# Four edits to a spectral transform with a gated feed-forward layer on one core: operand order, pieces of the inverse, the last pair, and the weights' ring

## The chip, the cores and the metric

The kernel runs on one core of one Trainium2 chip. The metric is the device time of one launch in microseconds (us): 2733.29 us as the median of three runs (2729.64 to 2734.06). All inputs and outputs are float32.

## The reference

The input x has 8 sequences of 3008 rows with 256 channels.

```python
X = np.fft.rfft(x, axis=1)
Yr = Xr @ w_r - Xi @ w_i + b_r          # 256 x 256 mixing, complex
Yi = Xr @ w_i + Xi @ w_r + b_i
Yr = np.sign(Yr) * np.maximum(np.abs(Yr) - 0.01, 0.0)   # the same for Yi
y = np.fft.irfft(Yr + 1j * Yi, n=3008, axis=1)
g, val = y @ w_gate, y @ w_val          # 24064 rows, 256 -> 1536
out = (g / (1 + np.exp(-g)) * val) @ w_out               # 1536 -> 256
```

## The kernel before

**Numbers in two parts.** Most products are made of three TensorE matmuls on `float32r` operands: each operand is held as an upper part (a rounded copy, made on ScalarE) and a lower part (the rest, a subtraction on VectorE or GpSimd), and upper x upper, upper x lower and lower x upper are added in PSUM. `PASSES` (L113) lists these as (weight part, data part). A matmul can start only when its part of the data is there, and the lower part is always made last.

**The transform (first some 620 us).** The transform of length 3008 = 47 x 64 is done in stages: `a_mm` (47 points), `b_mm` (64 points, for two of 24 frequencies at a time), mixing with w_r and w_i, shrinking, `bi_mm` (back over 64), `ai_mm` (back over 47). 96 steps, one for each pair of frequencies of each sequence, are overlapped: each function is recorded with a due time (`put(t, fn)`, step s plus an offset), and `go` issues the functions in the order of these times. Each engine then works through its own instructions in that order, and so does the queue of SyncE (SP), which starts all DMAs. In step s the order on TensorE is `b_mm` (s+0.23), `mix_mm` of the step before, `sum_mm` (s+1.0), `bi_mm` of an earlier step, and the `b_mm` of the next. The mixing takes three products instead of four: `sum_mm` multiplies Xr+Xi with w_r, VectorE adds the biases (`add_bias`), and `mix_mm` adds the two others, with w_i - w_r and -(w_i + w_r). These weights are made on the chip: `load_mix` reads w_r and w_i, `make_mix(0)` to `make_mix(2)` split them and their sums (`wm_hi`, `wm_lo`). The first sequence's `a_mm` results go through DRAM (`a_store`, then `load_a`).

**The layer.** 24 blocks of twice 512 rows (twice 384 in the last two) pass through six pairs of gate and value units. Both products, up and down, are made by Strassen's scheme in Winograd's form: seven products of blocks instead of eight, each of three matmuls. `gate_or_value` issues one unit: seven up products (`up`) into banks b1, b2, b3, and between them the down products of the pair before (`down`). The gate goes through Silu on ScalarE (`take`), the value is multiplied in on VectorE, and the four hidden blocks H11, H12, H22, H21 and four differences T1 to T4 are split by `upper` (ScalarE) and `lower` (GpSimd, or VectorE where named so). Up weights come by DMA, seven blocks for each unit, into a ring of four tiles (`wup`), which lies at the right end of SBUF. Down weights (`wdn`) stay in SBUF.

**Pieces of the inverse.** Six of eight sequences are finished before the layer starts. For the other two, 32 pieces of `ai_mm` (`inverse`, eight short matmul records each) are issued in the layer, in gate units, after the up product 7 and ahead of the up product 3. They use bank b1, from which Silu reads H11 just before, and ScalarE copies the result out (`xt2`).

**The end.** After the last pair nothing is left to lie beside its down products: H21 and T1 to T4 are split, seven products follow, and `result` adds them up into four output blocks, each stored by its own DMA.

Of the kernel before, what the change touches and what calls it, by code (L numbers as in the profile page):

```python
# [43 lines left out]
FIRST_X = {2: -0.93, 3: -0.90, 4: -0.5}  # L44
W_FIRST, W_STEP = 2, 4.2
WARM = 5
GAPS = {1: (0.38,), 2: (0.38, 0.78), 3: (0.38, 0.78, 0.90), 4: (0.38, 0.40, 0.78, 0.90), 5: (0.36, 0.38, 0.40, 0.78, 0.90)}
AFTER = {0.36: 0.62, 0.38: 0.63, 0.40: 0.64, 0.78: 1.03, 0.90: 1.15}

# [59 lines left out]
def f32(ap):  # L109
    return ap.bitcast(F32)  # L110


PASSES = ((0, 0), (0, 1), (1, 0))  # L113


@with_exitstack
def spectral_ffn(ctx: ExitStack, tc: tile.TileContext, xp, w_r, w_i, cb, wup_raw, wdn_raw, ca, cf, ci, co, out):
    nc = tc.nc
    const = ctx.enter_context(tc.tile_pool(name="const", bufs=1))
    dram = ctx.enter_context(tc.tile_pool(name="dram", bufs=2, space=DRAM))  # L120
    wdn = [const.tile([P, NQ, 7, P], F32R, name=f"wdn_{p}") for p in ("hi", "lo")]
    first = ctx.enter_context(tc.tile_pool(name="first", bufs=7, reuse_waits="tile"))
    xt_d = [dram.tile([P, 2, SEQ], F32, name=f"xt_d{b}", bufs=1) for b in range(B)]
    d2 = {b: dram.tile([NK, P, C], F32, name=f"d2_{b}", bufs=1) for b in range(B)}
    wup_d = [dram.tile([P, 2, 7 * P], F32, name=f"wup_d{u}", bufs=1) for u in range(2 * NQ)]
    front = ctx.enter_context(tc.tile_pool(name="front", bufs=1))
    ps_ = ctx.enter_context(tc.tile_pool(name="ps", bufs=1, space=PSUM))
    tail = ExitStack()
    last = tail.enter_context(tc.tile_pool(name="last", bufs=2, side="right"))
    one = ExitStack()  # L130
    ffn = FFN(ctx, tc, first, front, ps_, co, wdn, wup_d, xt_d, d2, out)
    engines = {nc.tensor.engine, nc.vector.engine, nc.scalar.engine, nc.gpsimd.engine}
    with tc.manual_schedule(engines=engines):
        with tc.manual_schedule(engines={nc.sync.engine}):
            go = transform(one, tc, front, last, tail, ffn, ps_, xp, w_r, w_i, cb, wup_raw, wdn_raw, ca, cf, ci, co, wdn, wup_d, xt_d, d2)
        ffn.run(go, one)


def transform(ctx, tc, front, last, tail, ffn, ps_, xp, w_r, w_i, cb, wup_raw, wdn_raw, ca, cf, ci, co, wdn, wup_d, xt_d, d2):
    nc = tc.nc  # L140
    v, act, g = nc.vector, nc.scalar, nc.gpsimd

# [75 lines left out]
    def weight_unit(i, at):  # L218
        kind, u = ("up", i) if i < 2 * NQ else ("down", i - 2 * NQ)
        src = wup_raw[u] if kind == "up" else wdn_raw[u]  # L220
        e = scratch[:, 2 * T : 3 * T].bitcast(I32)
        w = scratch[:, : 2 * T].rearrange("p (a b) -> p a b", b=P)
        a = w[:, 0:4, :].rearrange("p a b -> p (a b)")
        m = w[:, 4:8, :].rearrange("p a b -> p (a b)")
        box = {}
        high = lambda: box["raw"][:, :, 1]
        low = lambda: box["raw"][:, :, 0]

        def load():
            box["raw"] = last.tile([P, T, 2], I32, name="raw64", tag="z_in", bufs=3)  # L230
            nc.sync.dma_start(box["raw"].rearrange("p a b -> p (a b)"), src)

        steps = (
            lambda: v.tensor_scalar(e, high(), 20, 0x7FF, op0=ALU.logical_shift_right, op1=ALU.bitwise_and),
            lambda: v.tensor_scalar(e, e, 896.0, 1150.0, op0=ALU.max, op1=ALU.min),
            lambda: v.tensor_scalar(e, e, 896.0, float(1 << 23), op0=ALU.subtract, op1=ALU.mult),
            lambda: v.scalar_tensor_tensor(a.bitcast(I32), high(), -(1 << 31), e, op0=ALU.bitwise_and, op1=ALU.bitwise_or),
            lambda: v.tensor_scalar(e, high(), 0xFFFFF, 0x100000, op0=ALU.bitwise_and, op1=ALU.bitwise_or),
            lambda: v.tensor_scalar(m.bitcast(I32), low(), 8, None, op0=ALU.logical_shift_right),
            lambda: v.scalar_tensor_tensor(m, m.bitcast(I32), 2.0**-24, e, op0=ALU.mult, op1=ALU.add),  # L240
            lambda: v.scalar_tensor_tensor(a, m, 2.0**-20, a, op0=ALU.mult, op1=ALU.mult),
        )
        a21, a11, a12, a22, s1, s2, s3, s4 = [w[:, j, :] for j in range(8)]

        def sums():
            g.tensor_tensor(s1, a21, a22, op=ALU.add)
            g.tensor_tensor(s2, s1, a11, op=ALU.subtract)
            g.tensor_tensor(s3, a11, a21, op=ALU.subtract)
            g.tensor_tensor(s4, a12, s2, op=ALU.subtract)

        def upper():
            if kind == "up":
                box["both"] = sb.tile([P, 2, 7, P], F32R, name="both", tag="both", bufs=1)
                box["hi"], box["lo"] = box["both"][:, 0], box["both"][:, 1]
            else:
                box["hi"], box["lo"] = [part[:, u] for part in wdn]
            act.copy(box["hi"], w[:, 1:8, :])

        def lower():
            g.tensor_tensor(box["lo"], w[:, 1:8, :], f32(box["hi"]), op=ALU.subtract)  # L260

        def store():
            if kind == "up":
                nc.sync.dma_start(wup_d[u], f32(box["both"].rearrange("p i n a -> p i (n a)")))

        put(at - 1.5, load)
        for step, t in zip(steps, (0.39, 0.93, 0.96, 1.39, 1.93, 1.96, 2.39, 2.93)):
            put(at + t, step)
        put(at + 3.36, sums)
        put(at + 3.72, upper)  # L270
        put(at + 4.36, lower)
        put(at + 4.8, store)

# [80 lines left out]
    def sum_mm(b, p):  # L354
        ps = st["s", b, p] = ps_.tile([P, T], F32, name="ps_s")
        n = 0
        for cc in range(2):
            for w, x in PASSES:
                nc.tensor.matmul(ps[:, :C], lhsT=st["f", b, p][x][:, 2, cc, :], rhs=wmix[0][w][:, cc, :], start=n == 0, stop=n == 5)
                n += 1  # L360

# [47 lines left out]
    def bi_mm(b, p):  # L409
        parts = st.pop(("y", b, p))  # L410
        ps = st["z", b, p] = ps_.tile([P, T], F32, name="ps_z")
        if p == 0:
            for k in range(2):
                for n, (w, x) in enumerate(PASSES):
                    nc.tensor.matmul(ps[:, k * C : (k + 1) * C], lhsT=wi[w][:, k, :], rhs=parts[x][:, k * C : (k + 1) * C], start=n == 0, stop=n == 2)
        else:
            for n, (w, x) in enumerate(PASSES):
                nc.tensor.matmul(ps, lhsT=wi[w][:, 1, :], rhs=parts[x], start=n == 0, stop=n == 2)

    def z_out(b, p):  # L420
# [123 lines left out]
    put(-0.88, load_bias)  # L544
    put(-0.87, load_inverse)
    put(-0.20, make_mix, 0)
    put(0.84, make_mix, 1)
    put(0.86, make_mix, 2)
    put(-0.98, load_wf, 0)
    put(-0.97, load_mix)  # L550
    put(0.82, make_bias)
    put(0.88, make_inverse)

# [9 lines left out]
class FFN:  # L563
# [1 line left out]
    SUMS = ((4, 0, 1), (6, 2, 4), (5, 2, 0), (7, 3, 6))  # L565
    X_AT = {1: 1, 5: 4, 6: 6, 2: 3, 7: 5, 3: 2, 4: 7}

    def __init__(self, ctx, tc, first, front, ps_, co, wdn, wup_d, xt_d, d2, out):
        self.ctx, self.tc, self.first, self.front, self.ps_, self.co, self.wdn = ctx, tc, first, front, ps_, co, wdn
        self.wup_d, self.xt_d, self.d2, self.out = wup_d, xt_d, d2, out  # L570
        self.units = [n * NQ + q for q in range(NQ) for n in range(2)]
        self.held, self.xs, self.raws, self.made = {}, {}, {}, 0
        self.sb = None

    def open_ring(self):
        self.ring = self.ctx.enter_context(self.tc.tile_pool(name="ring", bufs=RING, side="right", reuse_waits="tile"))

    def load_unit(self, k):
# [35 lines left out]
    def run(self, go, one):  # L614
# [52 lines left out]
        def result(pair):  # L667
# [24 lines left out]
            store(2, 2)  # L692
            yield "after d5"

        ends = {}

        def step(name):
# [6 lines left out]
        def gate_or_value(pair, last, n, k, extra):  # L704
# [4 lines left out]
            m5 = hidden[:, 4 + n, :h]  # L709
            first = last is not None and last["q"] == 0  # L710
            closing = last is not None and last["q"] == NQ - 1

            def up(bank, n_, start):
                weights = [held[k][:, i, A_AT[n_], :] for i in range(2)]
# [63 lines left out]
            if gate:  # L778
                diff(last, T4, H21, T2)
                add(last, 1)  # L780
                if (blk, q) in pieces:
                    inverse()
            up(b2, 3, False)
            take(H22, last_sum)
            take(H12, b2[:, :h])
            done(3)
            if n:
                upper(pair, H22)
                lower(g, pair, H22)
            if gate:  # L790
                upper(last, T4)
                lower(g, last, T4)
# [5 lines left out]
                    step("after d2")  # L798
            if value:
                down(last, 5)  # L800
            up(b3, 4, False)
            take(H21, b3[:, :h])

# [75 lines left out]
                    total.update({n_: room(tag) for n_, tag in zip((3, 2, 5, 4), ("mixb1", "ps_z", "ps_x0", "ps_x1"))})  # L879
                last = pair  # L880
        upper(last, H21)
        lower(g, last, H21)
        for i, a, b in ((T1, H12, H11), (T2, H22, T1), (T3, H22, H12), (T4, H21, T2)):
            diff(last, i, a, b)
            upper(last, i)
            lower(g if i == T3 else v, last, i)
        ends["now"] = result(last)
        for n_ in (1, 3, 2, 5, 6, 4, 7):
            down(last, n_)
            if n_ in SUM_AT:  # L890
                add(last, n_)
            if n_ in (2, 6):
                step(f"after d{n_}")
        step("after d7")
        step("after d5")


_OUT = (P, 2, B * SEQ)
# [43 lines left out]
```

## Time and profile before

| what | value |
|---|---|
| median of three runs | 2733.29 us (2729.64 to 2734.06) |
| the profiled execution | 2734.88 us, its span on the core 2733.1 us |
| mean granted TensorE clock | 0.995 of 2.4 GHz |
| TensorE (PE) busy | 2693.9 us, 13173 matmul records |
| VectorE (DVE), ScalarE (ACT), GpSimd (POOL) busy | 2061.1, 1745.3, 1919.3 us |
| DMA | 493.05 MB, queue busy 55.1% of 16 engines |

In a timeline a row has start and duration in us, engine, line of the source, operation, result<-operands and the count of merged instructions; in brackets stands how long the engine had been idle before it and which instruction ended that. Matmuls overlap, so that the distance of two starts, not the duration, is what one costs. PEld is the loading of weights, which runs under the matmul before it.

### The profile page before, as it was taken

The numbers are of one execution on the slowest core, as the hardware profiler recorded it, in microseconds if no ns is written. First come the engines' busy times: TensorE is split into PE (matmuls) and PEld (weight loads), VectorE is DVE, ScalarE is ACT, GpSimd is POOL, SyncE is SP. The second block draws the span as 40 slices with busy tenths as digits, with TensorE's granted clock in tenths as the row PEclk, the third lists the DMA queues.
The fourth block names the chain that finished last, engine by engine and source line by source line (L and its number), as shares of the span: only waits on it lengthen the run. The fifth ranks groups of instructions, "written<-read, shape, count | busy, mean of one in ns | idle before, by whom it ended". The sixth has DMA issues, their size and how long they took to land. (4 is left out here: it accounts for less than half of the span.)

```text
span 2733.1 us, 39899 instructions
## 1 busy us (share of the span) xinstructions
PE 2693.9 (99%) x13173; PEld 2205.8 (81%) x13173; DVE 2061.1 (75%) x3108; ACT 1745.3 (64%) x3376; POOL 1919.3 (70%) x1460
## 2 busy tenths in 40 slices
PE   8999999999999999999999999999999999999998
PEld 5787878987888887888888888888888888888898
DVE  4888887667777777777777777777777777778787
ACT  5777777776666565656666566656665566565664
POOL 1333333247888788888888878888888888888885
PEclk9999999999999999999999999999999999999999
DMA  8998988873444454445444444445444444444453
GB/s 265 308 297 285 291 253 258 261 244 133 161 163 150 151 166 160 154 140 166 160 153 147 160 166 155 147 164 166 148 147 159 155 149 148 143 165 149 145 182 101
DMA packets 184990, 493.05 MB, mean 180 GB/s; under 512 B 17776, under 2 KB 93680, under 8 KB 184688
## 3 DMA queue, kind: packets, MB, share of 16 engines
q1 hardware_dynamic: 184784, 490.50, 55.1%
q8 instruction: 105, 1.72, 0.3%
q14 instruction: 101, 0.83, 0.1%
HBM read 379.81 MB, written 110.62 MB: 179 GB/s over the span
## 5 line engine op out<-in xcount | busy, mean ns | idle before, releaser
L624 PE MATMUL bank<-x_parts,wup 128*128 128x512 f32 (+1 forms) x6048 | 1552.4, 391 | 0.3 <-DVE bank L753 0.2
L624 PEld LDWEIGHTS bank<-x_parts,wup 128*128 128x128 f32 x6048 | 1128.0, 188 | 249.6 <-DVE bank L753 0.8
L644 POOL TENSOR_TENSOR h_parts<-more,h_parts 128x512 fp32r<-128x512 f32 (+1 forms) x573 | 853.4, 1500 | 140.6 <-ACT h_parts L640 125.4
L644 POOL TENSOR_TENSOR h_parts<-hidden,h_parts 128x512 fp32r<-128x512 f32 (+1 forms) x432 | 556.7, 1294 | 240.4 <-ACT h_parts L640 183.2
L624 PE MATMUL bank<-h_parts,wdn_hi 128*128 128x512 f32 (+1 forms) x2016 | 622.2, 389 | 0.9 <-POOL h_parts L644 0.9
L640 ACT CAST h_parts<-hidden 128x512 fp32r<-128x512 f32 (+1 forms) x432 | 265.4, 614 | 469.7 <-DVE hidden L726 469.7
L665 DVE TENSOR_TENSOR sums<-sums,bank 128x512 f32<-128x512 f32 (+1 forms) x360 | 242.3, 673 | 285.1 <-PE bank L624 284.0
L624 PEld LDWEIGHTS bank<-h_parts,wdn_hi 128*128 128x128 f32 x2016 | 378.6, 188 | 81.4 <-POOL h_parts L644 1.8
L726 DVE TENSOR_TENSOR hidden<-hidden,bank 128x512 f32<-128x512 f32 (+1 forms) x576 | 376.0, 674 | 87.8 <-PE bank L624 71.6
L396 POOL TENSOR_TENSOR t<-t,y 128x512 f32<-128x512 f32 x96 | 122.2, 1273 | 396.6 <-DVE y L393 389.3
L624 PE MATMUL bank<-h_parts,wdn_lo 128*128 128x512 f32 (+1 forms) x1008 | 392.6, 389 | 4.2 <-DVE sums L665 4.2
L640 ACT CAST h_parts<-more 128x512 fp32r<-128x512 f32 (+1 forms) x576 | 350.7, 609 | 21.4 <-DVE more L635 18.3
L724 ACT ACTIVATE hidden<-bank 128x512 f32<-128x512 f32 (+1 forms) x432 | 252.5, 584 | 142.9 <-PE bank L624 131.9
L635 DVE TENSOR_TENSOR more<-hidden 128x512 f32<-128x512 f32 (+1 forms) x288 | 281.5, 1015 | 0.0
L635 DVE TENSOR_TENSOR more<-hidden,more 128x512 f32<-128x512 f32 (+1 forms) x288 | 246.0, 854 | 0.0
L753 DVE TENSOR_TENSOR bank<-hidden,bank 128x512 f32<-128x512 f32 (+1 forms) x288 | 197.0, 684 | 55.9 <-PE bank L624 39.9
L731 ACT COPY bank<-bank 128x512 f32<-128x512 f32 (+1 forms) x288 | 161.6, 561 | 120.0 <-DVE hidden L726 110.5
L624 PEld LDWEIGHTS bank<-h_parts,wdn_lo 128*128 128x128 f32 x1008 | 189.6, 188 | 46.0 <-issue 4.5
L612 POOL TENSOR_TENSOR x_parts<-xf,x_parts 128x512 fp32r<-128x512 f32 (+1 forms) x168 | 211.3, 1278 | 22.0 <-ACT x_parts L611 22.0
L739 ACT COPY hidden<-bank 128x512 f32<-128x512 f32 (+1 forms) x288 | 166.9, 579 | 8.6 <-PE bank L624 0.4
L389 ACT COPY t<-mixb 64x256 f32<-64x256 f32 x384 | 140.7, 366 | 36.4 <-PE mixb L373 32.7
L776 DVE TENSOR_TENSOR hidden<-hidden,bank 128x512 f32<-128x512 f32 (+1 forms) x144 | 97.4, 676 | 56.8 <-PE bank L624 56.4
(95 smaller groups left out, 3153.0 us busy)
## 6 DMA issues: line engine op xcount, KB each, us to landing
wup<-wup_d SPq DMA_DIRECT2D x288, 896.0 KB, 4.7
d<-a SPq DMA_DIRECT2D x128, 192.0 KB, 3.9
a_in<-d SPq DMA_DIRECT2D x96, 256.0 KB, 4.9
d<-z SPq DMA_DIRECT2D x96, 256.0 KB, 4.7
out<-o SPq DMA_DIRECT2D x88, 256.0 KB, 6.2
scratch<-xp SPq DMA_DIRECT2D x116, 192.0 KB, 4.7
z_in<-d SPq DMA_DIRECT2D x48, 384.0 KB, 4.9
xt_d<-xt SPq DMA_DIRECT2D x48, 376.0 KB, 4.1
```

Of the source, the lines that this page charges most:

```text
L389: act.copy(t[64 * half : 64 * half + 64, k * C : (k + 1) * C], mixed[p % 2][64 * k : 64 * k + 64, half * C : (half + 1) * C])
L612: self.tc.nc.gpsimd.tensor_tensor(part[:, 1, :h], src, f32(part[:, 0, :h]), op=ALU.subtract)
L624: nc.tensor.matmul(o, lhsT=weights[w], rhs=parts[x], start=start and i == 0, stop=stop and i == 2, skip_group_check=True)
L635: v.tensor_tensor(at(o, h), at(a, h), at(b, h), op=ALU.subtract)
L640: act.copy(pair[i][:, 0, :h], at(i, h))
L644: eng.tensor_tensor(pair[i][:, 1, :h], at(i, h), f32(pair[i][:, 0, :h]), op=ALU.subtract)
L665: v.tensor_tensor(o, o, spare[:, :h], op=ALU.add)
L724: act.activation(at(i, h), src, AF.Silu)
L726: v.tensor_tensor(at(i, h), at(i, h), src, op=ALU.mult)
L731: act.copy(b3[:, :h], b1[:, :h])
L739: act.copy(m5, b2[:, :h])
L753: v.tensor_tensor(b2[:, :h], m5, b3[:, :h], op=ALU.add)
```

## The change

Five things change.

1. The order of the three matmuls in `sum_mm` and `bi_mm` (`LATE`): those with the lower part of the data come last, in `sum_mm` after both halves of the contraction.
2. At the start w_r and w_i are loaded behind the first `a_in`, and all three sets of mixing weights are made before the first step's other work.
3. The pieces of the inverse are issued one product later, after the up product 3.
4. The last pair's down goes by eight plain products on H11, H22, H12, H21 instead of seven of Strassen's. For that block a21 of the last pair's down weights is kept too (`w21`, 1 KB beside `wdn`), H12 is split as well, its lower part on VectorE.
5. A pad of 864 bytes stands beside the ring, which moves down by as much; `w21` moves what lies left up by 1024 bytes.

```diff
+PAD = 216
+LATE = ((0, 0), (1, 0), (0, 1))
...
+    w21 = const.tile([P, 2, P], F32R, name="w21")
...
             act.copy(box["hi"], w[:, 1:8, :])
+            if i == 3 * NQ - 1:
+                act.copy(w21[:, 0, :], a21)
...
             g.tensor_tensor(box["lo"], w[:, 1:8, :], f32(box["hi"]), op=ALU.subtract)
+            if i == 3 * NQ - 1:
+                g.tensor_tensor(w21[:, 1, :], a21, f32(w21[:, 0, :]), op=ALU.subtract)
...
-        for cc in range(2):
-            for w, x in PASSES:
+        for w, x in LATE:
+            for cc in range(2):
                 nc.tensor.matmul(ps[:, :C], lhsT=st["f", b, p][x][:, 2, cc, :], rhs=wmix[0][w][:, cc, :], start=n == 0, stop=n == 5)
...
-            for n, (w, x) in enumerate(PASSES):
+            for n, (w, x) in enumerate(LATE):
                 nc.tensor.matmul(ps, lhsT=wi[w][:, 1, :], rhs=parts[x], start=n == 0, stop=n == 2)
...
-    put(0.84, make_mix, 1)
-    put(0.86, make_mix, 2)
+    put(-0.18, make_mix, 1)
+    put(-0.16, make_mix, 2)
     put(-0.98, load_wf, 0)
-    put(-0.97, load_mix)
+    put(-0.945, load_mix)
...
     def open_ring(self):
+        self.ctx.enter_context(self.tc.tile_pool(name="pad", bufs=1, side="right")).tile([P, PAD], F32, name="pad")
         self.ring = ...
...
+        def outer(pair, c, n_):
+            h = pair["h"]
+            o = pair.setdefault("o", {})[c, 2] = self.sb.tile([P, T], F32, name="o", bufs=4)[:, :h]
+            v.tensor_tensor(o, pool["sums"][:, SUM_AT[n_], :h], total[5][:, :h], op=ALU.add)
...
             if gate:
                 diff(last, T4, H21, T2)
                 add(last, 1)
-                if (blk, q) in pieces:
-                    inverse()
             up(b2, 3, False)
             take(H22, last_sum)
             take(H12, b2[:, :h])
+            if gate and (blk, q) in pieces:
+                inverse()
...
                 lower(g, pair, H22)
+                if final:
+                    upper(pair, H12)
+                    lower(v, pair, H12)
...
+            if final and n:
+                outer(pair, 1, 6)
             up(b3, 4, False)
...
         upper(last, H21)
-        lower(g, last, H21)
-        for i, a, b in ((T1, H12, H11), (T2, H22, T1), (T3, H22, H12), (T4, H21, T2)):
-            diff(last, i, a, b)
-            upper(last, i)
-            lower(g if i == T3 else v, last, i)
-        ends["now"] = result(last)
-        for n_ in (1, 3, 2, 5, 6, 4, 7):
-            down(last, n_)
-            ...
+        outer(last, 2, 7)
+        lower(v, last, H21)
+        ...
+        def direct(i, f, j):
+            for c in (1, 2):
+                weights = [part[:, q, block[c, f], :] for part in wdn] if (c, f) in block else [self.w21[:, x, :] for x in range(2)]
+                product(bank[c, j][:, :h], weights, [last[i][:, x, :h] for x in range(2)], (c, j, f) == (2, 2, 2), i in (H12, H21))
+
+        def close(c, j, left):
+            v.tensor_tensor(o[c, j], left, bank[c, j][:, :h], op=ALU.add)
+            s = BLOCKS[-1][0] + (h if j == 1 else 0)
+            nc.sync.dma_start(out[:, c - 1, s : s + h], o[c, j])
+
+        direct(H11, 1, 1)
+        direct(H22, 2, 2)
+        direct(H12, 1, 2)
+        close(1, 2, o[1, 2])
+        close(2, 2, o[2, 2])
+        direct(H21, 2, 1)
+        close(1, 1, sums(1))
+        close(2, 1, sums(7))
```

On VectorE, at the start of the program before the change (`wm` are parts of mixing weights, `wsum` their sums, `f` the spectrum of a step, `wi` the inverse's table, `mixb` the bank that the biases open):

```order
L206 TENSOR_TENSOR wm_lo<-wr,wm_hi 128x512
L338 TENSOR_TENSOR f<-ps_b,f 128x256
L344 CAST f_hi<-f 128x256
L347 TENSOR_TENSOR f_lo<-f,f_hi 128x256
L350 TENSOR_TENSOR f_lo<-ps_b,f_hi 128x512
L211 TENSOR_SCALAR bias<-bias 32x256 x2
L201 TENSOR_TENSOR wsum<-wj,wr 128x512
L206 TENSOR_TENSOR wm_lo<-wsum,wm_hi 128x512
L203 TENSOR_TENSOR wsum<-wj,wr 128x512
L204 TENSOR_SCALAR wsum<-wsum 128x512
L206 TENSOR_TENSOR wm_lo<-wsum,wm_hi 128x512
L215 TENSOR_TENSOR wi_lo<-raw_i,wi_hi 128x256
```

The same place after it:

```order
L209 TENSOR_TENSOR wm_lo<-wr,wm_hi 128x512
L204 TENSOR_TENSOR wsum<-wj,wr 128x512
L209 TENSOR_TENSOR wm_lo<-wsum,wm_hi 128x512
L206 TENSOR_TENSOR wsum<-wj,wr 128x512
L207 TENSOR_SCALAR wsum<-wsum 128x512
L209 TENSOR_TENSOR wm_lo<-wsum,wm_hi 128x512
L345 TENSOR_TENSOR f<-ps_b,f 128x256
L351 CAST f_hi<-f 128x256
L354 TENSOR_TENSOR f_lo<-f,f_hi 128x256
L357 TENSOR_TENSOR f_lo<-ps_b,f_hi 128x512
L214 TENSOR_SCALAR bias<-bias 32x256 x2
L218 TENSOR_TENSOR wi_lo<-raw_i,wi_hi 128x256
```

The five instructions of the second and third set of mixing weights moved from behind the first step's spectrum to ahead of it.

On TensorE, `sum_mm` and `bi_mm` of a step of the transform before (`f_lo` and `y_lo` are the lower parts of the data):

```order
L359 MATMUL ps_s<-wm_hi,f_hi 128x256
L359 MATMUL ps_s<-wm_hi,f_lo 128x256
L359 MATMUL ps_s<-wm_lo,f_hi 128x256
L359 MATMUL ps_s<-wm_hi,f_hi 128x256
L359 MATMUL ps_s<-wm_hi,f_lo 128x256
L359 MATMUL ps_s<-wm_lo,f_hi 128x256
L418 MATMUL ps_z<-y_hi,wi_hi 128x512
L418 MATMUL ps_z<-y_lo,wi_hi 128x512
L418 MATMUL ps_z<-y_hi,wi_lo 128x512
```

And after:

```order
L366 MATMUL ps_s<-wm_hi,f_hi 128x256 x2
L366 MATMUL ps_s<-wm_lo,f_hi 128x256 x2
L366 MATMUL ps_s<-wm_hi,f_lo 128x256 x2
L425 MATMUL ps_z<-y_hi,wi_hi 128x512
L425 MATMUL ps_z<-y_hi,wi_lo 128x512
L425 MATMUL ps_z<-y_lo,wi_hi 128x512
```

`f_lo` is now asked for at the fifth of six matmuls instead of the second, and `y_lo` at the third of three instead of the second.

## Rows read from the trace of the kernel before

**Rows 1.** Windows: busy us (count) of PE, PEld, DVE, ACT, POOL; clock; DMA share; GB/s.
```profile
2160.00:2500.00 340.00, 340.00 (x1465) 275.00 (x1464) 263.34 (x367) 210.43 (x378) 288.26 (x208) 1.00 0.44 148
...
42.50:46.00 3.50, 3.22 (x13) 3.01 (x14) 1.78 (x5) 0.73 (x3) 0.00 (x0) 0.51 0.87 255
```

**Rows 2.** Timeline of the start: DMA issues on SP, then PE, then DVE.
```profile
24.55 0.41 SPq L186 DMA_DIRECT2D wj<-w_i  x1
25.07 0.93 SPq L312 DMA_DIRECT2D a_in<-d  x2
...
31.75 2.05 PE L320 MATMUL ps_b<-wf,a_in 128*128 128x128 f32 x8 [2.21 <-DMA a_in<-d]
42.78 0.55 PE L373 MATMUL mixb<-wm_hi,f_hi 128*128 128x256 f32 x1 [3.29 <-DVE mixb L364]
...
34.72 0.42 DVE L338 TENSOR_TENSOR f<-ps_b,f 128x256 f32<-128x256 f32 x1 [3.29 <-ACT f_hi L341]
36.57 0.59 DVE L211 TENSOR_SCALAR bias<-bias 32x256 f32<-32x256 f32 x2
37.19 0.69 DVE L201 TENSOR_TENSOR wsum<-wj,wr 128x512 f32<-128x512 f32 x1
41.61 0.42 DVE L215 TENSOR_TENSOR wi_lo<-raw_i,wi_hi 128x256 fp32r<-128x256 f32 x1
41.94 0.69 DVE L364 TENSOR_TENSOR mixb<-ps_s,bias 128x512 f32<-128x512 f32 x1
```

**Rows 3.** DMA issues: tensors, queue, count, size, median us from issue to landing.
```profile
wj<-w_i SPq DMA_DIRECT2D x1, 256.0 KB, 5.8
```

**Rows 4.** Waits from 60 to 620 us: total us, times, longest.
```profile
PEld ps_z L418 <- DVE y_lo L405: 16.9, 39, 0.9
```

**Rows 5.** Timeline of PE: one `bi_mm` that waits.
```profile
178.75 0.39 PE L418 MATMUL ps_z<-y_hi,wi_hi 128*128 128x512 f32 x1
179.25 0.50 PE L418 MATMUL ps_z<-y_lo,wi_hi 128*128 128x512 f32 x1
179.59 0.40 PE L418 MATMUL ps_z<-y_hi,wi_lo 128*128 128x512 f32 x1
```

**Rows 6.** Timeline round one piece of the inverse: PE, then ACT.
```profile
731.99 1.13 PE L824 MATMUL bank<-w,z 96*128 96x94 f32 x8
...
731.34 0.60 ACT L724 ACTIVATE hidden<-bank 128x512 f32<-128x512 f32 x1 [1.12 <-PE bank L624]
...
733.16 0.48 ACT L833 COPY xt<-bank 128x376 f32<-128x376 f32 x1 [0.71 <-PE bank L824]
```

**Rows 7.** Waits from 650 to 2150 us.
```profile
PEld bank L824 <- ACT hidden L724: 15.5, 32, 0.5
```

**Rows 8.** Timeline of the end: PE, ACT, POOL, DVE.
```profile
2715.99 0.51 PE L624 MATMUL bank<-h_parts,wdn_hi 128*128 128x384 f32 x2
2723.73 0.66 PE L624 MATMUL bank<-h_parts,wdn_lo 128*128 128x384 f32 x1 [4.21 <-DVE sums L665]
...
2715.62 0.52 ACT L640 CAST h_parts<-hidden 128x384 fp32r<-128x384 f32 x1 [1.12 <-DVE hidden L726]
...
2716.21 2.28 POOL L644 TENSOR_TENSOR h_parts<-hidden,h_parts 128x384 fp32r<-128x384 f32 x2 [0.63 <-ACT h_parts L640]
...
2715.03 1.54 DVE L726 TENSOR_TENSOR hidden<-hidden,bank 128x384 f32<-128x384 f32 x3
2716.49 1.14 DVE L635 TENSOR_TENSOR more<-hidden 128x384 f32<-128x384 f32 x1
...
2718.83 0.55 DVE L635 TENSOR_TENSOR more<-hidden,more 128x384 f32<-128x384 f32 x1
...
2728.57 0.55 DVE L675 TENSOR_TENSOR o<-sums,bank 128x384 f32<-128x384 f32 x1
```

**Rows 9.** Groups by line and shape: count, busy us, mean ns of one, idle before.
```profile
L624 PE MATMUL bank<-x_parts,wup 128*128 128x512 f32 x5544 | 1449.8, 396 | 0.3 <-DVE bank L753 0.2
...
L624 PE MATMUL bank<-h_parts,wdn_hi 128*128 128x512 f32 x1848 | 577.4, 393 | 0.0
```

More of the change, by code (lines that the diff above doesn't have):

```diff
@@ L130, in spectral_ffn @@
     one = ExitStack()
-    ffn = FFN(ctx, tc, first, front, ps_, co, wdn, wup_d, xt_d, d2, out)
+    ffn = FFN(ctx, tc, first, front, ps_, co, wdn, w21, wup_d, xt_d, d2, out)
     engines = {nc.tensor.engine, nc.vector.engine, nc.scalar.engine, nc.gpsimd.engine}
@@ L134, in spectral_ffn, with transform @@
         with tc.manual_schedule(engines={nc.sync.engine}):
-            go = transform(one, tc, front, last, tail, ffn, ps_, xp, w_r, w_i, cb, wup_raw, wdn_raw, ca, cf, ci, co, wdn, wup_d, xt_d, d2)
+            go = transform(one, tc, front, last, tail, ffn, ps_, xp, w_r, w_i, cb, wup_raw, wdn_raw, ca, cf, ci, co, wdn, w21, wup_d, xt_d, d2)
         ffn.run(go, one)
-def transform(ctx, tc, front, last, tail, ffn, ps_, xp, w_r, w_i, cb, wup_raw, wdn_raw, ca, cf, ci, co, wdn, wup_d, xt_d, d2):
+def transform(ctx, tc, front, last, tail, ffn, ps_, xp, w_r, w_i, cb, wup_raw, wdn_raw, ca, cf, ci, co, wdn, w21, wup_d, xt_d, d2):
     nc = tc.nc
@@ L413, in bi_mm @@
             for k in range(2):
-                for n, (w, x) in enumerate(PASSES):
+                for n, (w, x) in enumerate(LATE):
                     nc.tensor.matmul(ps[:, k * C : (k + 1) * C], lhsT=wi[w][:, k, :], rhs=parts[x][:, k * C : (k + 1) * C], start=n == 0, stop=n == 2)
         else:
-            for n, (w, x) in enumerate(PASSES):
+            for n, (w, x) in enumerate(LATE):
                 nc.tensor.matmul(ps, lhsT=wi[w][:, 1, :], rhs=parts[x], start=n == 0, stop=n == 2)
@@ L566, with __init__ @@
     X_AT = {1: 1, 5: 4, 6: 6, 2: 3, 7: 5, 3: 2, 4: 7}
-    def __init__(self, ctx, tc, first, front, ps_, co, wdn, wup_d, xt_d, d2, out):
+    def __init__(self, ctx, tc, first, front, ps_, co, wdn, w21, wup_d, xt_d, d2, out):
         self.ctx, self.tc, self.first, self.front, self.ps_, self.co, self.wdn = ctx, tc, first, front, ps_, co, wdn
@@ L572, in __init__ @@
         self.held, self.xs, self.raws, self.made = {}, {}, {}, 0
-        self.sb = None
+        self.w21, self.sb = w21, None
     def open_ring(self):
+        self.ctx.enter_context(self.tc.tile_pool(name="pad", bufs=1, side="right")).tile([P, PAD], F32, name="pad")
         self.ring = self.ctx.enter_context(self.tc.tile_pool(name="ring", bufs=RING, side="right", reuse_waits="tile"))
@@ L711, in gate_or_value @@
             closing = last is not None and last["q"] == NQ - 1
+            final = blk == len(BLOCKS) - 1 and q == NQ - 1
             def up(bank, n_, start):
@@ L881, in run @@
         upper(last, H21)
-        lower(g, last, H21)
-        for i, a, b in ((T1, H12, H11), (T2, H22, T1), (T3, H22, H12), (T4, H21, T2)):
-            diff(last, i, a, b)
-            upper(last, i)
-            lower(g if i == T3 else v, last, i)
-        ends["now"] = result(last)
-        for n_ in (1, 3, 2, 5, 6, 4, 7):
-            down(last, n_)
[L890 to L895, printed above, removed]
+        outer(last, 2, 7)
+        lower(v, last, H21)
+        h, q = last["h"], last["q"]
+        sums = lambda n_: pool["sums"][:, SUM_AT[n_], :h]
+        bank = {(1, 1): total[2], (1, 2): total[3], (2, 1): total[4], (2, 2): spare}
+        block = {(1, 1): A_AT[1], (1, 2): A_AT[2], (2, 2): A_AT[4]}
+        o = last["o"]
+        for c in (1, 2):
+            o[c, 1] = self.sb.tile([P, T], F32, name="o", bufs=4)[:, :h]
+        def direct(i, f, j):
+            for c in (1, 2):
+                weights = [part[:, q, block[c, f], :] for part in wdn] if (c, f) in block else [self.w21[:, x, :] for x in range(2)]
[12 more added lines that the diff above has]
+        close(2, 1, sums(7))
 _OUT = (P, 2, B * SEQ)
```

## The prediction, made before the changed kernel ran

> **What bounds the kernel now.** I read the windows first. In a stretch of the layer where only full products run, PE is busy for 340.00 of 340 us at full clock and gets through 1465 matmuls, one each 0.232 us; DMA is at 0.44 [rows 1]. So the layer, three quarters of the time, is a queue of matmuls without gaps, and only a gap that PE really has, or a cheaper matmul, can be won there. The change leaves the number of matmuls nearly alone (three more of 384 columns at the end), so the rest of the reading was a search for gaps of PE in the places that the edits touch: the timeline of the start [rows 2], the waits of the transform with one timeline [rows 4, 5], the waits of the layer with one piece [rows 6, 7], and the timeline of the end [rows 8]. The reader is to see in each which instruction ends the gap and how much of it PE could have filled.
>
> **Start: mixing weights.** Before, the first mixing matmul stands at 42.78 us, after PE had idled 3.29 us for VectorE's biases, which stand at 41.94. VectorE did the first spectrum from 34.72 to 36.57, the biases' signs (0.59), and then, from 37.19 to 41.61, the two sums of mixing weights with their splitting: 4.4 us, in which it also waits for ScalarE [rows 2]. That block now goes first, from the time w_j lands. It was issued at 24.55 and took 5.8 us [rows 2, 3], so it landed at 30.35; it now stands behind one `a_in`, and `a_in` cannot be issued before the last store has landed. Two issues there took 0.93 us, and 256 KB go by in about 1 us at such a rate, so I put w_j at 31.5. The block then ends at about 36.0, the spectrum takes 1.85 (to 37.9), a wait for ScalarE's copies some 0.2, signs and `wi_lo` 1.0 (0.59 + 0.42), and the biases start at 39.2 to 39.6; the mixing starts 0.84 behind that (as 42.78 behind 41.94), at about 40.2. That is 2.5 us earlier. PE worked at 1.2 GHz from 42.50 to 46.00, busy for 3.22 us [rows 1], after that idle time; without it the same work needs half, 1.6 us less. The first `b_mm`, which waited 2.21 us for `a_in` [rows 2], starts sooner, but its results now wait on ScalarE behind the weights. I take 3.0 us: the 2.5, and a third of the 1.6, because other, shorter idle times are still there. From both sides: 4.1 if the clock stays up all the while, 1.0 if w_j lands 1.5 us later than I put it.
>
> **Transform: the lower part last.** In the stretch 60 to 620 us the loading of `bi_mm`'s second weights waits 39 times for `y_lo`, 16.9 us in all, 0.43 on the mean [rows 4]. One of them: starts at 178.75, 179.25, 179.59 [rows 5], so the second comes 0.50 behind the first where 0.23 is due [rows 1]. With the two last exchanged PE fills this wait with one matmul of 512 columns, 0.232 us, and still waits 0.2 after it. 39 x 0.232 = 9.0 us. In `sum_mm` the new order lets PE start three matmuls of 256 columns more before it asks for `f_lo`. I count that at nothing: VectorE makes `y_lo` right behind `f_lo`, so where `sum_mm` would run on, `bi_mm` waits as much longer for the same `y_lo`. What comes next on PE, `b_mm`, moves up by the 0.232, and the spectrum of the next step with it. The bounds are 0 (VectorE or the DMA queue sets the pace and the time comes back as another wait) and 16.9 (the whole wait). I take 9.0, which is worked out from the rows where it happens.
>
> **Pieces.** 32 times the loading of the inverse's operand waits 0.49 us for Silu on H11 [rows 7] (15.5 / 32), because only one up product, 0.7 us, lies between Silu's input and bank b1's next writer. The timeline shows Silu from 731.34 to 731.94 and the piece at 731.99 [rows 6]. With another product of three matmuls between, 0.7 us, the wait is gone. What PE loses is less than the wait, as some of it lay under the matmul before: the matmul ahead of the piece started at about 731.53, the next was due at 731.76, so 0.23 is seen, and the refilling of the pipeline costs a part of a matmul more. I take 0.28, 32 x 0.28 = 9.0 us, between 7.4 (0.23 each) and 15.5. What is late next: ScalarE's copy out of b1 (0.48) now stands behind both other Silus and ahead of T4's split. The piece takes 0.9 us, and after it PE has two products, 1.4 us, before value's first product writes b1; copy and hand-over need about 0.8 from the piece's end. Some 0.4 to 0.6 are left, and T4 is asked for two products later still. So the copy stays covered.
>
> **End.** Before, PE stands still for 4.21 us until 2723.73 for the chain of differences, and VectorE's last sum starts at 2728.57 [rows 8], 4.5 us before the span's end. Now: H12 is multiplied by 2716.1 (the second of three from 2715.03). ScalarE splits H22 from 2715.62 (0.52) and H12 to 2716.65. VectorE's lower part of H12 runs beside GpSimd's of H22 (two from 2716.21, 2.28 together). Next to GpSimd a VectorE difference took 1.14 us, alone 0.55 [rows 8]; I take 1.14, to 2717.8. Then follow the first outer sum (0.5), H21's product (0.5), the second outer sum, H21's upper part on ScalarE at 2718.85 to 2719.4 and its lower part to 2719.95. PE passes through 24 matmuls at 0.17 to 0.175 ([rows 8]: two take 0.51, of which 0.34 is the second's own) from 2715.8, waits a little for H22's and H21's lower parts, and starts the last at 2720.6. The last sum starts at 2721.3 instead of 2728.57. I take 7.2 us; bounds 6.0 (four stores close together, or ScalarE slower) and 8.0 (the difference takes 0.55).
>
> The Trainium skill ("SBUF — State Buffer", section "Who interferes with whom") says that a VectorE instruction with two SBUF inputs and a GpSimd one that reads SBUF exclude each other, the later one waiting until the other ends; this speaks against giving H12's lower part to VectorE. The 1.14 against 0.55 agrees in kind. By the rule alone the difference would begin only when H22's is done, at 2717.3, and end at 2717.9: the end would win 7.1 instead of 7.2.
>
> **Pad.** The ring and all that lies left move, no instruction does. The ring's matmuls are listed at 396 ns, those with resident weights at 393 [rows 9]; no row shows the ring elsewhere. I take nothing, between 5544 x 3 ns = 17 us won (the ring becomes as the resident ones) and as much lost. The extra splitting of one weight block is one short ScalarE and GpSimd instruction in the transform: nothing, as PE does not wait for it.
>
> **Sum.** 3.0 + 9.0 + 9.0 + 7.2 = 28.2 us off the profiled execution's 2734.88, 2706.7; that execution lies 1.6 above the median of the runs, so the median comes to 2733.29 - 28.2 = 2705.1.
>
> **Rivals.**
> *The pad helps.* If the ring's distance to the resident weights' address matters, the 5544 matmuls fall by 2 to 3 ns each, 11 to 17 us: 2688 to 2694. For it: the 3 ns. Against: these are durations, which overlap, and the data come from other tiles as well. Chance 0.18.
> *The transform keeps its pace.* If the loop over VectorE and ScalarE, or the DMA queue, sets the steps, the 9.0 and most of the 3.0 come back as other waits: 2705 + 11 = 2716. For it: each waiting `bi_mm` follows one long chain on VectorE. Against: PE's next `b_mm`, at which that chain begins again, does move. The same time results, for other reasons, if the copy from b1 comes too late and the pieces win nothing: 2714. Together 0.14.
> *The new place slows the ring.* If weights read from the new address cost more, each of 6048 up matmuls pays: the gains are gone from 28.2 / 6048 = 4.7 ns each, a fiftieth of 0.232; at 8 ns the time is 2705 + 48 = 2753. For it: nothing but that both groups differ by 3 ns. Chance 0.04.
> *The edits do nothing measurable*, since the waits only change names: 2733. Chance 0.03.
>
> **How the numbers follow.** The forecast has 0.61 and its own range is 2698 to 2711. What this kernel's measurement can tell from no change is 0.2%, 5.5 us. The range from 2689 to 2716 takes in most of the pad's case and of the slower transform. Faster: 0.61 + 0.18 + 0.14 = 0.93; same 0.03; slower 0.04.
>
> **What would show it.** The first mixing matmul at about 40 us, and no half clock behind it; the waits for `y_lo` halved, not gone; no wait of the inverse's operand for Silu, and none of value's first product for the copy; less than 1 us of idle PE in the end, and the last sum 7 us sooner; in the stretch of full products still 0.232 us each. The forecast is wrong if this last number moves, if the layer starts less than 8 us sooner, or if value's first product waits.

## The result, and the profile after

The changed kernel takes 2661.47 us (median of four runs, 2658.75 to 2665.69). Its ratio to the kernel before (2732.39 us, now the median of four) is 0.9743, 95% interval 0.9726 to 0.9760. That is 71 us off, where 28 were forecast, and below the range that was given. Of the four terms that were priced, the transform came out at about half its size, the other three near theirs, and together they came near the forecast's sum; the term that was put at zero, the pad, was worth some 46 us.

The windows of the changed kernel, one stretch of full products and the start (columns as in [rows 1]):

```profile
2110.00:2445.00 335.00, 335.00 (x1477) 276.70 (x1476) 269.33 (x371) 208.89 (x377) 287.55 (x208) 1.00 0.45 153
...
42.50:46.00 3.50, 3.50 (x23) 2.69 (x22) 2.34 (x5) 3.07 (x8) 1.27 (x1) 1.00 0.57 159
```

PE was busy without a gap before and is so now, at the same granted clock of 1.00. Yet 1477 matmuls go through in 335 us, one each 226.8 ns, where 1465 took 340 us, 232.1 ns each [rows 1]. In the second row the stretch behind the first mixing now has the full clock. That need not be a gain: the half clock lies elsewhere now, as the account of the start below shows.

The two traces are split at four landmarks that both have: the first `mix_mm`, the first up product, the first up products of 384 columns, the last up product. Timeline of PE, the kernel before (its first `mix_mm` stands in [rows 2]), then after:

```profile
609.46 0.85 PE L624 MATMUL bank<-x_parts,wup 128*128 128x512 f32 x3
...
2580.10 1.91 PE L624 MATMUL bank<-x_parts,wup 128*128 128x512 f32 x9
...
2715.29 0.69 PE L624 MATMUL bank<-x_parts,wup 128*128 128x384 f32 x3
```

```profile
40.30 0.68 PE L380 MATMUL mixb<-wm_hi,f_hi 128*128 128x256 f32 x1
...
599.62 0.86 PE L632 MATMUL bank<-x_parts,wup 128*128 128x512 f32 x3
...
2514.64 1.73 PE L632 MATMUL bank<-x_parts,wup 128*128 128x512 f32 x8
...
2649.82 0.51 PE L632 MATMUL bank<-x_parts,wup 128*128 128x384 f32 x2
```

| stretch | before | after | gain |
|---|---|---|---|
| to the first `mix_mm` | 42.78 | 40.30 | 2.5 |
| from there to the first up product | 566.7 | 559.3 | 7.4 |
| from there to the row that leads into 384 columns | 1970.6 | 1915.0 | 55.6 |
| from there to the last up matmul | 135.5 | 135.4 | 0.1 |
| from the last up matmul to the span's end | 17.5 | 9.1 | 8.4 |

The first two rows are from one execution each, and executions differ there by several us. The first up product starts at 604.5 to 609.5 in the four traces with the old start and transform (before, e1, e2 and e3 of the experiments below), and at 597.5 to 602.1 in those with the new ones, except for e4 with 608.0. The last up matmul is the last of its row (2715.64 and 2650.00); the spans' ends are 2733.1 and 2659.1. Of the 55.6 us, 10.3 lie at the pieces (below). The other 45 are 5.4 ns on each of some 8300 products of 512 columns (5544 and 1848 in [rows 9], and half of the latter again for the lower part of the weights).

Groups by line and shape in the changed kernel, 700 to 2440 us (columns as in [rows 9]):

```profile
L632 PE MATMUL bank<-x_parts,wup 128*128 128x512 f32 x5029 | 1277.7, 389 | 0.0
L632 PE MATMUL bank<-h_parts,wdn_hi 128*128 128x512 f32 x1676 | 516.4, 389 | 0.0
```

Products with resident weights fell from 393 to 389 ns although those weights did not move. Their starts say the same: the three matmuls of such a product started 230.6 and 231.9 ns apart on the mean before, and 226.7 and 226.9 now (all such products in 2130 to 2470 us). A place of the ring that costs something costs it to the matmuls next to the ring's own, too.

The 384-column blocks gained next to nothing. Windows of 100 us there, before and after:

```profile
2590.00:2690.00 100.00, 100.00 (x566) 98.11 (x565) 82.54 (x144) 63.15 (x142) 79.70 (x74) 1.00 0.55 180
```

```profile
2530.00:2630.00 100.00, 100.00 (x569) 98.48 (x568) 82.85 (x145) 63.64 (x143) 79.94 (x74) 1.00 0.56 182
```

176.7 and 175.7 ns each: what the old place cost appears with 512 columns, hardly with 384.

### The profile page after: what moved, and what is told of

It is laid out like the page before. It is cut to its first block, busy times and chain, and to the rows that moved or that the text cites. A ratio compares the mean times of both kernels' runs of the same rounds, so it can differ in the third digit from the quotient of the medians.

```text
span 2659.1 us, 39894 instructions
## 1 busy us (share of the span) xinstructions
PE 2632.8 (99%) x13176; PEld 2201.3 (83%) x13176; DVE 2075.1 (78%) x3101; ACT 1742.5 (66%) x3374; POOL 1919.4 (72%) x1459
## 4 chain that ended last, share of the span: by engine, by line
PE 92%; DVE 4%; ACT 2%; DMA 1%; issue 1%; SPq 0%; POOL 0%; DVEq 0%; ACTq 0%; POOLq 0%
PE bank L632 76%; PE mixb L380 3%; PE ps_a L305 3%; PE ps_x L450 3%; PE ps_b L327 2%; PE ps_z L425 2%; PE ps_s L366 2%; PE bank L843 1%; DVE f_hi L351 1%; DMA scratch<-xp 1%; DVE y_lo L412 1%; DVE f_lo L357 1%; ACT t L396 1%; DVE f_lo L354 0%; ACT f_hi L348 0%
## 5 line engine op out<-in xcount | busy, mean ns | idle before, releaser
L632 PE MATMUL bank<-x_parts,wup 128*128 128x512 f32 (+1 forms) x6048 | 1511.9, 385 | 0.3 <-DVE bank L767 0.2
L632 PE MATMUL bank<-h_parts,wdn_hi 128*128 128x512 f32 (+1 forms) x2014 | 612.3, 385 | 0.0
L740 DVE TENSOR_TENSOR hidden<-hidden,bank 128x512 f32<-128x512 f32 (+1 forms) x576 | 375.9, 674 | 78.2 <-PE bank L632 69.5
L643 DVE TENSOR_TENSOR more<-hidden 128x512 f32<-128x512 f32 (+1 forms) x286 | 288.8, 1048 | 0.0
L643 DVE TENSOR_TENSOR more<-hidden,more 128x512 f32<-128x512 f32 (+1 forms) x286 | 255.3, 893 | 0.0
L380 PE MATMUL mixb<-wm_hi,f_hi 128*128 128x256 f32 x384 | 131.8, 343 | 1.4 <-DVE mixb L371 1.3
```

What stands on the lines that cost most here:

```text
L380: nc.tensor.matmul(mixed[p % 2][:, half * C : (half + 1) * C], lhsT=parts[x][:, q, cc, :], rhs=wmix[i][w][:, cc, :], start=False, stop=(cc ...
L632: nc.tensor.matmul(o, lhsT=weights[w], rhs=parts[x], start=start and i == 0, stop=stop and i == 2, skip_group_check=True)
L643: v.tensor_tensor(at(o, h), at(a, h), at(b, h), op=ALU.subtract)
L740: v.tensor_tensor(at(i, h), at(i, h), src, op=ALU.mult)
```

## The experiments

All times are medians of four to ten runs; each ratio is to the kernel before on the same chip, whose median was 2735.81 beside e1 to e4, 2734.84 beside e5 to e8 and 2734.49 beside e9 to e12.

| run | ring's start, within 256 bytes | inputs and resident weights, within 256 | other edits | us | ratio (95%) |
|---|---|---|---|---|---|
| e1 pad only | 199808, 128 | 128 | none | 2689.97 | 0.9824 (0.9809 to 0.9839) |
| e2 32 bytes | 200640, 192 | 128 | none | 2735.37 | 0.9997 (0.9987 to 1.0007) |
| e3 block only | 200672, 224 | 128 | none | 2735.08 | 0.9999 (0.9989 to 1.0010) |
| e4 no pad | 200672, 224 | 128 | all | 2711.26 | 0.9909 (0.9890 to 0.9927) |
| e5 352 | 200320, 128 | 128 | all | 2662.44 | 0.9734 (0.9719 to 0.9748) |
| e6 608 | 200064, 128 | 128 | all | 2661.51 | 0.9731 (0.9714 to 0.9747) |
| e7 736 | 199936, 0 | 128 | all | 2706.74 | 0.9895 (0.9880 to 0.9909) |
| e8 800 | 199872, 192 | 128 | all | 2709.34 | 0.9904 (0.9889 to 0.9919) |
| e9 | 199936, 0 | 0 | all | 2660.09 | 0.9729 (0.9715 to 0.9744) |
| e10 | 200064, 128 | 0 | all | 2707.00 | 0.9900 (0.9886 to 0.9915) |
| e11 old order | 199808, 128 | 128 | without LATE | 2666.54 | 0.9755 (0.9740 to 0.9769) |
| e12 old mix | 199808, 128 | 128 | without the mix weights' move | 2665.59 | 0.9752 (0.9735 to 0.9768) |

The starts are those that the allocation gives; a ring tile is 7168 bytes, 28 x 256, so all four tiles have the same remainder.

**Which edit, and which address.** The change moves two things: the ring by 864 bytes, and inputs and hidden blocks by 1024 (`w21`). e1 and e3 do one each, e2 tries another pad, e4 leaves the pad out.

```diff
 # e1: the kernel before, and (e2: PAD = 8)
+PAD = 216
+        self.ctx.enter_context(self.tc.tile_pool(name="pad", bufs=1, side="right")).tile([P, PAD], F32, name="pad")
 # e3: the kernel before, and
+    const.tile([P, 2, P], F32R, name="w21")
 # e4: the changed kernel
-PAD = 216
-        self.ctx.enter_context(self.tc.tile_pool(name="pad", bufs=1, side="right")).tile([P, PAD], F32, name="pad")
```

> The kernel before with the pad of 864 bytes alone: the ring starts at byte 199808 of a partition instead of 200672 and all else stays. Theory A (the ring's address makes every product of the layer slow, whichever weights it uses itself): the 512-column products start 227 ns apart instead of 232.4, about 45 us off, near 2688. Theory B (it is the addresses of the inputs, which the new weight block moves up by 1024 bytes): nothing changes, 2732. Theory C (neither alone, both must agree): 2732 here and in the run with the block alone.

> The kernel before with a pad of 32 bytes: the ring starts at 200640, again a multiple of 64, but at another place within 512 and 2048 bytes than with 864. Theory A in the form that the multiple of 64 decides: 2688, as with 864 bytes. Theory A in the form that the distance to the inputs or a place within a larger block decides: the time differs from that of the pad of 864, 2700 to 2735. Theory B: 2732.

> The kernel before with 1024 bytes more below the inputs, as the new weight block takes them; the ring stays at 200672. Theory A: 2732, products 232 ns apart. Theory B: 2688, products 227 ns apart.

> The changed kernel without the pad: the inputs stay 1024 bytes up, the ring is back at 200672. Theory A: the 45 us come back, 2706, which would be the prediction's own number for the other three edits. Theory B: 2661. Theory C: 2706, too, and then the first and third run tell it from A.

One window, 2130 to 2470 us, of e1, e2, e3 and e4 in this order:

```profile
2130.00:2470.00 340.00, 340.00 (x1500) 280.90 (x1500) 273.80 (x377) 215.09 (x387) 291.09 (x210) 1.00 0.45 151
```

```profile
2130.00:2470.00 340.00, 339.95 (x1467) 273.62 (x1466) 263.44 (x368) 209.31 (x376) 283.69 (x205) 1.00 0.45 150
```

```profile
2130.00:2470.00 340.00, 339.95 (x1468) 274.88 (x1467) 263.84 (x368) 209.33 (x376) 284.32 (x205) 1.00 0.45 150
```

```profile
2130.00:2470.00 340.00, 340.00 (x1460) 274.01 (x1459) 264.05 (x369) 207.86 (x372) 282.82 (x205) 1.00 0.45 150
```

Only e1 has 1500 matmuls in 340 us, 226.7 ns each. The pad alone takes 45.8 us off (2735.81 to 2689.97); the block alone and 32 bytes do nothing. Theory A holds, theories B and C fall, and 200640, a multiple of 64, shows that a multiple of 64 is not enough. The count behind PE is the instrument for all that follows. e4 came to 24.6 us less than before, not far from the forecast's sum, 28.2, in which the pad has no part.

**Which remainder counts.** Four pads in the changed kernel, `PAD = 88, 152, 184, 200` (352, 608, 736 and 800 bytes).

> The changed kernel with a pad of 352 bytes: the ring starts at 200320, the same place within 512 bytes as with 864 (128), but another within 1024 and 2048. Theory 128 (a start that is a multiple of 128 is enough), theory 256 (128 within 256) and theory 512 (128 within 512, where the inputs and the resident weights start as well): 2661, products 227 ns apart. Theory 1024 or 2048 (the place within a larger block): about 2711, 232 ns or more.

> The changed kernel with a pad of 608 bytes: the ring starts at 384 within 512 bytes, 128 within 256. Theories 128 and 256: 2661. Theory 512: about 2711.

> The changed kernel with a pad of 736 bytes: the ring starts at 256 within 512 bytes, 0 within 256 and within 128. Theory 128: 2661. Theories 256 and 512: about 2711.

> The changed kernel with a pad of 800 bytes: the ring starts at 192 within 512 bytes, 64 within 128, a multiple of 64 and of nothing larger. All theories that ask for a multiple of 128 or more: about 2711. A theory in which only the places 448 and 480 within 512 bytes, which the kernel before and the run with 32 bytes had, are bad: 2661.

The same window of e6 and of e7:

```profile
2130.00:2470.00 340.00, 340.00 (x1500) 281.06 (x1499) 273.70 (x376) 214.90 (x387) 290.80 (x211) 1.00 0.45 154
```

```profile
2130.00:2470.00 340.00, 340.00 (x1465) 275.13 (x1464) 262.98 (x369) 208.77 (x374) 284.70 (x206) 1.00 0.44 147
```

352 and 608 bytes are as fast as 864, 736 and 800 as slow as none. 608 stands at 384 within 512, so 512 falls; 736 is a multiple of 128, so 128 falls. What is left is 128 within 256 bytes. e7 and e8, with a bad place and all other edits, are 28.1 and 25.5 us below before: again about the sum of the other terms.

**Place or distance.** All of x_parts, h_parts and wdn start at 128 within 256 as well. e9 and e10 put 128 bytes below them, so that they start at 0, and the ring at 0 and at 128.

```diff
 # the changed kernel; e9 with PAD = 184, e10 with PAD = 152
+    const.tile([P, 32], F32, name="shift")
     wdn = [const.tile([P, NQ, 7, P], F32R, name=f"wdn_{p}") for p in ("hi", "lo")]
```

> The changed kernel with 128 bytes put below the resident weights, which moves these and the inputs to 0 within 256 bytes, and a pad of 736, with which the ring too stands at 0 within 256. Theory R (what counts is the distance: ring, resident weights and inputs must stand at the same place within 256 bytes): 2661, products 227 ns apart. Theory P (the place itself counts, weights must stand at 128 within 256): 2707 or later, with the products of both kinds of weights at 232 or more.

> The same shift of 128 bytes below the resident weights, but a pad of 608, so that the ring stands at 128 within 256 bytes while inputs and resident weights stand at 0. Theory R: about 2707, 232 to 233 ns. Theory P: the up products, two thirds, are fast, those with resident weights slow: about 2676.

e9, then e10:

```profile
2130.00:2470.00 340.00, 340.00 (x1500) 280.98 (x1499) 273.72 (x378) 213.74 (x385) 291.55 (x211) 1.00 0.46 153
```

```profile
2130.00:2470.00 340.00, 340.00 (x1466) 275.11 (x1465) 262.43 (x367) 210.00 (x378) 283.96 (x206) 1.00 0.45 149
```

The ring at 0 was slow in e7 and is fast in e9; at 128 it was fast in e6 and is slow in e10. So it is the distance: theory R holds, theory P falls. The ring is fast when its start has the same remainder within 256 bytes as the starts of the inputs and the resident weights, and slow at the distances of 64, 96 and 128 bytes that were tried; smaller ones were not. Two things stay open. Inputs and resident weights always had one remainder (the shift moved all that lies left of the ring), so that it is not shown with which of them the ring must agree. And by what means a wrong distance slows the matmuls is not shown by any record: loads take 187 to 188 ns in either case, only the starts of the matmuls come later, and products with resident weights are slowed as well, although their own weights and inputs have the same remainder in every run.

**The other terms.**

```diff
 # e11: the changed kernel
-LATE = ((0, 0), (1, 0), (0, 1))
+LATE = PASSES
-        for w, x in LATE:
-            for cc in range(2):
+        for cc in range(2):
+            for w, x in LATE:
 # e12: the changed kernel
-    put(-0.18, make_mix, 1)
-    put(-0.16, make_mix, 2)
+    put(0.84, make_mix, 1)
+    put(0.86, make_mix, 2)
-    put(-0.945, load_mix)
+    put(-0.97, load_mix)
```

> The changed kernel with the old order of the three products in sum_mm and bi_mm, the lower part second. By the prediction's term for this edit: 9.0 us slower, 2670. If the transform keeps VectorE's pace and most of it returned as other waits: 2661 to 2664. By the sum of the starts in the two traces (from the first mixing matmul to the first product of the layer 566.7 us before, 559.3 after): 7 us, 2668.

> The changed kernel with w_j issued and the mixing weights made where they were before. By the prediction's term: 3.0 us slower, 2664, the first mixing matmul near 42.8 instead of 40.3 and PE at half clock again behind it. If the transform takes the start back: 2661.

The old order costs 6.5 us against e9, its neighbour on the same chip, which differs from the changed kernel only in where things lie; the runs of the two do not overlap. Against the changed kernel, which was timed at another time, it costs 5.1 us by the medians, and 3.0 when each is taken against its own kernel before. The old mix weights cost 5.5, 4.1 and 2.0 us in the same three ways. The traces of all runs give a figure for the order that does not hang on one neighbour: from the first `mix_mm` to the first up product it is 564.7 us on the mean of five traces with the old order (562.4 to 566.7) and 559.8 on the mean of nine with the new one (558.2 to 562.7), 4.9 us less. So of e11's expectations neither the 9 us nor a return of nearly all came; the 7 us, taken from one trace of each kernel, were somewhat high.

Of e12's expectations the time and the first `mix_mm`, at 42.25, came about as expected, but not the half clock behind it:

```profile
42.50:46.00 3.50, 3.50 (x27) 2.99 (x27) 1.76 (x5) 1.95 (x5) 0.00 (x0) 1.00 0.82 261
```

Waits on PEld from 60 to 605 us, in e11 and in the changed kernel:

```profile
PEld ps_z L425 <- DVE y_lo L412: 14.9, 35, 0.9
...
PEld mixb L380 <- DVE mixb L371: 6.2, 18, 1.2
...
PEld ps_s L366 <- DVE f_lo L354: 5.2, 24, 0.3
```

```profile
PEld ps_z L425 <- DVE y_lo L412: 18.2, 36, 1.1
...
PEld mixb L380 <- DVE mixb L371: 10.1, 25, 1.4
```

With the new order the wait for `f_lo` is gone, the wait for `y_lo` is longer, and that of `mix_mm` for the biases grew by 3.9 us and 7 times. I read it so: in the wait for `y_lo` PE gets there earlier and waits for the same end of VectorE's chain, and in the wait for the biases VectorE takes back a part of what was won.

## Why the prediction was wrong

**The pad is the step that failed:** "I take nothing, between 5544 x 3 ns = 17 us won ... and as much lost". It was worth 45.8 us alone (e1). The price was read from [rows 9], as the difference of the ring's matmuls to those with resident weights, on the view that the latter show a good place. They do not: they run between the ring's and were slowed by them, 393 ns to 389 now. So the effect was nearly double per matmul (5.4 ns of start-to-start distance instead of 3), and it hit all of some 8300 products instead of 5544. The rival "the pad helps" had the right sign and place and the same too small size, 11 to 17 us. The reading was blind in another way, too: a stretch in which PE is busy for 340.00 of 340 us was taken for a stretch where nothing can be won. It showed that PE never waits for an instruction, not that a matmul costs what it must. The two shapes gave no alarm: 232.1 and 176.7 ns are 0.453 and 0.460 ns for each column. What the trace did hold are the single starts: equal matmuls that wait for nothing stood 226 to 238 ns apart, and 226.8 is the pace that all of them have now. The distances are a hint and no measure of what can be won: in e7, with the ring in a bad place, some of these distances are 224, less than any run has on the mean, and in e2 the ring's products stand evenly 233 or 234 apart.

The four bad-place runs with all edits (e4, e7, e8, e10) took 24.6, 28.1, 25.5 and 27.5 us off; 28.2 was the sum.

**Start, 3.0: the 2.5 us came as forecast, the share of the clock is not borne out.** The first `mix_mm` stands at 40.30, forecast about 40.2. VectorE after, the steps whose times were worked out:

```profile
31.67 0.69 DVE L204 TENSOR_TENSOR wsum<-wj,wr 128x512 f32<-128x512 f32 x1 [0.33 <-DMA wj<-w_i]
...
35.48 0.69 DVE L209 TENSOR_TENSOR wm_lo<-wsum,wm_hi 128x512 fp32r<-128x512 f32 x1 [0.69 <-ACT wm_hi L208]
36.24 0.42 DVE L345 TENSOR_TENSOR f<-ps_b,f 128x256 f32<-128x256 f32 x1
...
39.08 0.70 DVE L371 TENSOR_TENSOR mixb<-ps_s,bias 128x512 f32<-128x512 f32 x1
```

w_j landed at about 31.6 (forecast 31.5), the block ended at 36.2 (36.0), the biases began at 39.08 (39.2 to 39.6). Undoing it costs 2.0 to 5.5 us (e12). In e4's trace w_j was issued at 30.55 instead of 25.74, and the first `mix_mm` stood at 45.37: the lateness of w_j, for which the lower bound stood, does occur.

The half clock did not go away, it lies elsewhere. Windows, before and then after:

```profile
25.40:35.70 10.30, 7.65 (x15) 3.71 (x16) 1.60 (x4) 2.56 (x6) 0.00 (x0) 0.50 1.01 286
```

```profile
25.40:39.10 13.70, 11.33 (x26) 6.30 (x27) 6.51 (x14) 5.04 (x10) 0.00 (x0) 0.50 0.99 315
```

In both kernels TensorE's clock fell to 1.2 GHz at about 25.4 us, while PE waited some 4 us for its input. Before, it rose at 35.7 and fell once more from 42.5 to 45.9, at the end of the 3.29 us of idle time; after, it stayed down until 39.1. That makes about 13.7 us of half clock in either kernel. Nor does the old place of the mixing weights bring the half clock behind the first mixing: with it, e1, e2 and e12 have 1.00 in 42.50 to 46.00 and only e3, like before, about half (0.54). So the third of 1.6 us that was added for the clock is shown by no run.

**Transform, 9.0: about half came,** 4.9 us by the traces, 3.0 to 6.5 by e11's times. The step "PE's next `b_mm` moves up by the 0.232, and the spectrum of the next step with it" holds only where VectorE has time left. The timeline of VectorE after, one step:

```profile
169.73 0.42 DVE L400 TENSOR_SCALAR y<-t 128x512 f32<-128x512 f32 x1
170.07 0.69 DVE L371 TENSOR_TENSOR mixb<-ps_s,bias 128x512 f32<-128x512 f32 x1
170.67 1.45 DVE L240 SCALAR_TENSOR_TENSOR scratch<-raw,scratch 128x512 int32<-128x512 int32 x1
172.10 0.42 DVE L345 TENSOR_TENSOR f<-ps_b,f 128x256 f32<-128x256 f32 x1
...
175.10 0.42 DVE L400 TENSOR_SCALAR y<-t 128x512 f32<-128x512 f32 x1
```

From 169.73 to 175.10 VectorE has no gap: where it also converts a block of the layer's weights (`scratch`), its own work can fill the step, here 5.37 us. Between 60 and 605 us there are 22 such steps (with less than 0.1 us of gaps) of 91 in the changed kernel and 22 of 91 in e11, with 5.24 us on the mean in both, so PE's order changes nothing in them. The wait for `y_lo` did not halve, as the prediction wanted to see; it moved to `y_lo` from `f_lo` and on to the biases. This is the rival "the transform keeps its pace", in part of the steps.

**Pieces, 9.0: right, size 10.3.** Timeline of PE and ScalarE round one piece, after:

```profile
718.72 0.84 PE L632 MATMUL bank<-x_parts,wup 128*128 128x512 f32 x3
719.40 1.03 PE L843 MATMUL bank<-w,z 96*128 96x94 f32 x8
720.21 0.47 PE L632 MATMUL bank<-h_parts,wdn_lo 128*128 128x512 f32 x1
```

```profile
720.71 0.46 ACT L852 COPY xt<-bank 128x376 f32<-128x376 f32 x1
```

The piece starts 0.68 us behind the start of three products, without a wait. Over 32 pieces the distance from the product before to the piece's start fell from 445 to 229 ns and the piece itself from 914 to 810: 32 x 0.320 = 10.3 us. In e7, with the ring in a bad place, the two are 228 and 811, so that this gain owes nothing to the pad. No wait of value's first product for the copy appears: as forecast, it stayed covered.

**End, 7.2: mechanism right, size 8.4,** a little past the upper bound of 8.0. In the ten traces with the new end it takes 8.9 to 9.1 us from the last up matmul to the span's end, in the four with the old one 17.5. GpSimd and VectorE in the end, after:

```profile
2650.58 1.01 POOL L652 TENSOR_TENSOR h_parts<-hidden,h_parts 128x384 fp32r<-128x384 f32 x1 [0.62 <-ACT h_parts L648]
...
2651.07 0.94 DVE L652 TENSOR_TENSOR h_parts<-hidden,h_parts 128x384 fp32r<-128x384 f32 x1 [0.65 <-ACT h_parts L648]
...
2653.59 0.56 DVE L652 TENSOR_TENSOR h_parts<-hidden,h_parts 128x384 fp32r<-128x384 f32 x1 [0.18 <-ACT h_parts L648]
...
2654.99 1.01 DVE L917 TENSOR_TENSOR o<-sums,bank 128x384 f32<-128x384 f32 x2
```

The last sum (the second of the two, at 2655.5) starts 5.5 us behind the last up matmul, forecast 5.7. The rest of the gain is behind it: 3.6 us to the span's end, where 4.5 were left before [rows 8], which the sum held constant. The lower part beside GpSimd took 0.94, taken as 1.14. It began at 2651.07 with GpSimd's difference running from 2650.58 to 2651.59; 0.52 us of that were left, and a difference of VectorE alone takes 0.56 (2653.59). By the rule of the Trainium skill ("SBUF — State Buffer", section "Who interferes with whom"), that the two exclude each other, it would take until 1.08 us after its start. The 0.94 comes near this, and the wait appears as a longer duration and not as a later start.

## What to carry to other kernels

An engine that is busy without a gap can still be slow: look at the distances of equal instructions that wait for nothing, and where they differ, ask why. Even distances prove nothing, though (e2). Where weights are loaded under matmuls that stream from SBUF, try both at the same remainder within 256 bytes of the partition; here, with `float32r` operands, the wrong distance cost 5.4 ns of each 512-column product, 46 us in all, and a pad of some hundred bytes gave it back. And a comparison group that runs interleaved with the suspect is no baseline: shift the suspect's address instead, in a run of its own.

## What the runs showed of the hardware

- Distances of 64 (e2, e8), 96 (before, e3, e4) and 128 bytes (e7, e10) within 256 cost the same, 1460 to 1468 matmuls in 340 us; equal remainders (the other runs) gave 1500 or 1501. No step in between was seen.
- The cost depends on the columns: 5.4 ns at 512, about 1 ns at 384 (windows of before and after).
- Products whose own weights and inputs have the same remainder pay too, when they run between those of the ring (before against after).
- The slow pace is not noise but a fixed pattern: in the kernel before, starts of successive matmuls lie 226 to 238 ns apart, and the 63 matmuls of a pair of units take 14640 ns again and again, within a nanosecond in nearly all of the window from 2130 to 2470 us.
